# Attention output with V stationary and row sums apart, and the other arm of the final branch laid out next

## The chip, the cores and the metric

The kernel runs on one core of one Trainium2 chip. The metric is device time in microseconds (us) of one execution. A core has TensorE (PE, matmuls into PSUM), VectorE (DVE), ScalarE (ACT), GpSimd (POOL) and SyncE (SP, which issues most DMAs). Each runs its own instruction stream in order, and semaphores tie them together.

## The reference

One transformer block on 2048 tokens of width 1024, in bf16, with adaptive layer norm. Six vectors of 1024 come from `silu(c) @ w_mod`. There are 32 query heads and 4 key/value heads of 128; keys and values are the last W = 512 positions of a cache.

```python
h = _layernorm(x) * (1 + ca) + sa
q = (h @ wq), in 32 heads of 128
scores = einsum('bhqd,bhkd->bhqk', q, k) * 128 ** -0.5     # k: 512 positions, each kv head serves 8 heads
p = softmax(scores)
o = einsum('bhqk,bhkd->bhqd', p, v)
x = x + ga * (o, heads side by side) @ wo
h = _layernorm(x) * (1 + cb) + sb
x = x + gb * ((silu(h @ w_gate) * (h @ w_up)) @ w_down)     # inner width 3584
```

## The kernel before

There are two programs in one. `fast_path` computes everything with a softmax that subtracts no maximum, and beside it a bound on the scores; where the bound is too large a flag is set, and `general_path` computes the output again. The flag is read by every engine at the end (lines 1241 to 1243) and the usual value, 0, skips `general_path`.

`fast_path` cuts the 2048 tokens into four chunks of 512 columns. The attention stage is one loop (line 1203) over k = 0 to 128, where unit g is head g % 32 of chunk g // 32. In step k the program issues the scores of unit k (`emit_s`, line 1025), the query projection of unit k + 3 (`emit_q`, line 1015), whatever tasks a table holds for step k (`at`, line 806; filled in lines 1114 to 1147), and last the attention output of unit k - 1 (`emit_o`, line 1054). The tasks are layer norms, modulation rows, loads, the bound, and the output projection `emit_wo` (line 1090), one 128x512 result a step, from 13 steps after the first head of its group of eight on. The instruction order on each engine follows from this; a scheduler may move instructions that are not pinned.

Matmuls: `emit_q` 8 with 512 moving columns; `emit_s` 4, each 128 positions against 512 tokens, in two PSUM tiles of two banks, with one exponential on ACT for each into `pT` (512 positions by 512 tokens, positions on partitions); `emit_wo` 8.

`emit_o` takes each 128x128 block of `pT` as the stationary operand and lets V move: 128 columns of V and one column of ones (`v_sb` is loaded with room for it, lines 705 to 709). So 16 matmuls of 129 columns a head leave tokens on partitions, and column 128 holds the sum of the probabilities. Three results of 129 share a PSUM bank (`SLOTS`); `close_bank` (line 1042) takes the reciprocals of the sums and writes the scaled output as bf16 into `oq`. `xpose_o` (line 1077) turns `oq` by four DMA transposes a group of four heads, issued by SP, into `oT`, with the head's 128 values on partitions, which `emit_wo` uses as stationary operand.

Tiles of 512 columns in PSUM come from one ring of four banks (`mm`, line 649). In SBUF, pool `blkC` (line 634, 13 tiles) holds `oq`, `oT`, the `wo` tiles, and later the `wd` tiles of the down projection; `blkB` (7) holds `wq`, kT, `v_sb`, and later `wg` and `wu`; all weights are loaded by SP in program order (`load`, line 666).

After the attention stage come, for each chunk, 28 steps of gate and up (`emit_gu`, line 1161) and 8 of down (`emit_down`, line 1181). Line 779 is a form that matters below: the modulation rows as matmuls with 32 stationary columns, four of them to the four quarters of a bank's partitions.

Of the kernel before, what the change touches and what calls it, by code (L numbers as in the profile page):

```python
# [8 lines left out]
ACT = mybir.ActivationFunctionType  # L9
ALU = mybir.AluOpType  # L10
AX = mybir.AxisListType
BF16 = mybir.dt.bfloat16
FP32 = mybir.dt.float32
# [575 lines left out]
def fast_path(ctx, tc, flag, A_x, A_k_cache, A_v_cache, A_wq, A_wo, B_x, B_w_gate, B_w_up,  # L589
# [3 lines left out]
    nc = tc.nc  # L593
    P = 128
    _, S, D = A_x.shape
    _, Hkv, Sk, Dh = A_k_cache.shape
    HD = A_wq.shape[1]
    H = HD // Dh
# [4 lines left out]
    TCW = 512  # L603
    NTC = S // TCW
    QT = TCW // P
    DT = D // P
    FT = F // P
    WT = W // P
    DH = D // 512
    HQ = 8  # L610
    NQ = H // HQ
    NFG = FT // 4
    scale = float(Dh) ** -0.5
# [13 lines left out]
    v_v = A_v_cache[0][:, k0:k0 + W, :].rearrange("kv (j p) d -> p kv j d", p=P)  # L627
# [3 lines left out]
    hpool = ctx.enter_context(tc.tile_pool(name="hT", bufs=4))  # L631
    pa_ = ctx.enter_context(tc.tile_pool(name="blkA", bufs=8))
    pb_ = ctx.enter_context(tc.tile_pool(name="blkB", bufs=7))
    pc_ = ctx.enter_context(tc.tile_pool(name="blkC", bufs=13))
    wk = ctx.enter_context(tc.tile_pool(name="work", bufs=2))
    sm = ctx.enter_context(tc.tile_pool(name="small", bufs=4))
    psp = ctx.enter_context(tc.tile_pool(name="psum", bufs=4, space=bass.MemoryType.PSUM))
    dp = ctx.enter_context(tc.tile_pool(name="dram", bufs=4, space=bass.MemoryType.DRAM))

    def blkA(name, shape, dt=BF16):  # L640
        return pa_.tile(shape, dt, name=name, tag="A")

    def blkB(name, shape, dt=BF16):
        return pb_.tile(shape, dt, name=name, tag="B")

    def blkC(name, shape, dt=BF16):
        return pc_.tile(shape, dt, name=name, tag="C")

    def mm(name, shape=(P, 512), dt=FP32):
        return psp.tile(list(shape), dt, name=name, tag="mm", bufs=4)  # L650

    def big(name, shape=(P, 2, 512), dt=FP32):
        return psp.tile(list(shape), dt, name=name, tag="s", bufs=2)
# [6 lines left out]
    def pin(ins, what="steps"):  # L660
        return tc.keep_in_program_order(ins) if stage[what] else ins

    def fetch(out, in_):
        pin(nc.sync.dma_start(out=out, in_=in_), "dma")  # L664

    def load(out, in_):
        with nc.allow_non_contiguous_dma(reason="weight slice"):
            fetch(out=out, in_=in_)
# [20 lines left out]
    def load_wq(cc, hg, parts=(0, 1)):  # L689
        for i in parts:  # L690
            t = blkB("wq", [P, 4, 512])
            load(t, wq_v[:, 4 * i:4 * i + 4, hg * 512:(hg + 1) * 512])
            wq_tiles[(cc, hg, i)] = t
# [8 lines left out]
    for kv in range(Hkv):  # L702
        pin(nc.sync.dma_start_transpose(
            out=kT[:, kv, :], in_=A_k_cache[0, kv, k0:k0 + W, :]), "dma")
    VW = Dh + 4
    v_sb = blkB("v_sb", [P, Hkv, WT, VW])
    for kv in range(Hkv):
        load(v_sb[:, kv, :, 0:Dh], v_v[:, kv])
    nc.gpsimd.memset(v_sb[:, :, :, Dh:VW], 1.0)
    load_wq(0, 1)  # L710


# [2 lines left out]
    ones_bf = const.tile([P, P], BF16, name="ones_bf")  # L715
# [90 lines left out]
    def at(k, f, *a):  # L806
        tasks.setdefault(k, []).append((f, a))
# [115 lines left out]
    for t in range(QT):  # L923
        ln_stats(t)
        n = ln_norm(t, t % 2 == 0)
# [5 lines left out]
    for half in range(DH):  # L931
# [6 lines left out]
        for n in range(4 * LEAD):  # L938
            dt, g = (4 * half + n // LEAD, n % LEAD) if half == 0 else (4 + n % 4, n // 4)
            nc.tensor.matmul(q0_ps[g],  # L940
                             lhsT=wq_tiles[(0, 0, dt // 4)][:, dt % 4, g * P:(g + 1) * P],
                             rhs=hT[("h1", 0)][:, dt, :], start=(dt == 0), stop=(dt == DT - 1))
# [7 lines left out]

    def bound_wq(hg, i, j):
        w = wq_tiles[(1 + hg % (NTC - 1), hg, i)][:, 2 * j:2 * j + 2, :]
        junk = wk.tile([P, 2, 512], BF16, name="junk", tag="junk", bufs=1)
        col = (hg * 2 + i) * 2 + j
        pin(nc.vector.scalar_tensor_tensor(out=junk, in0=w, scalar=1.0, in1=w, op0=ALU.mult,
                                           op1=ALU.mult, accum_out=sq[:, col:col + 1]))
# [8 lines left out]
    def bound_k(kv):  # L965
        for j in range(WT):
            i = kv * WT + j
            junk = wk.tile([P, Dh], BF16, name="junk", tag="junk", bufs=1)
            src = k_ld[0][:, kv, j, :]
            pin(nc.vector.scalar_tensor_tensor(out=junk, in0=src, scalar=1.0, in1=src,  # L970
                                               op0=ALU.mult, op1=ALU.mult,
                                               accum_out=kk[:, i:i + 1]))
# [35 lines left out]
    NU = NTC * H  # L1008
    pT = {}
    oT = {}  # L1010
    oq = {}
    acc = {}
    wo_tiles = {}

# [10 lines left out]
    def emit_s(g):  # L1025
        kv = (g % H) // rep
        p = blkA("pT", [P, WT, TCW])
        for jj in range(WT // 2):
            s_ps = big("s_ps")
            for i in range(2):  # L1030
                j = 2 * jj + i
                nc.tensor.matmul(s_ps[:, i, :], lhsT=kT[:, kv, j * P:(j + 1) * P], rhs=qT[g],  # L1032
                                 start=True, stop=True)
            nc.scalar.activation(out=p[:, 2 * jj:2 * jj + 2, :], in_=s_ps, func=ACT.Exp,  # L1034
                                 scale=scale)
        del qT[g]
        pT[g] = p

    SLOTS = 3
    o_slot = {"n": 0, "runs": []}  # L1040

    def close_bank():
        ps, runs = o_slot["ps"], o_slot["runs"]
        n = o_slot["n"]
        rl = sm.tile([P, SLOTS], FP32, name="rl", tag="rl", bufs=4)
        nc.vector.reciprocal(out=rl[:, 0:n], in_=ps[:, 0:n, Dh])
        for g, t0, t1, s0 in runs:
            cnt = t1 - t0
            dst = oq[(g // H, (g % H) // 4)][:, t0:t1, g % 4, :]
            sc = rl[:, s0:s0 + cnt].unsqueeze(2).to_broadcast([P, cnt, Dh])  # L1050
            nc.vector.tensor_tensor(out=dst, in0=ps[:, s0:s0 + cnt, 0:Dh], in1=sc, op=ALU.mult)  # L1051
        o_slot.update(n=0, runs=[])

    def emit_o(g):
        cc, h = divmod(g, H)
        kv = h // rep
        if h % 4 == 0:
            oq[(cc, h // 4)] = blkC("oq", [P, QT, 4, Dh])
        for t in range(QT):
            if o_slot["n"] == 0:  # L1060
                o_slot["ps"] = mm("o_ps", (P, SLOTS, Dh + 1))
            s_ = o_slot["n"]
            for j in range(WT):
                nc.tensor.matmul(o_slot["ps"][:, s_, :], lhsT=pT[g][:, j, t * P:(t + 1) * P],  # L1064
                                 rhs=v_sb[:, kv, j, 0:Dh + 1], start=(j == 0),
                                 stop=(j == WT - 1))
            runs = o_slot["runs"]
            if runs and runs[-1][0] == g:
                runs[-1][2] = t + 1
            else:  # L1070
                runs.append([g, t, t + 1, s_])
            o_slot["n"] = s_ + 1
            if o_slot["n"] == SLOTS or (t == QT - 1 and h % HQ == HQ - 1):
                close_bank()
        del pT[g]

    def xpose_o(cc, hg):
        src = oq.pop((cc, hg))
        dst = oT[(cc, hg)] = blkC("oT", [P, 4, TCW])
        for t in range(QT):  # L1080
            pin(nc.sync.dma_start_transpose(
                out=dst[:, :, t * P:(t + 1) * P],
                in_=src[:, t, :, :].rearrange("p h d -> p (h d)")), "dma")

    def load_wo(cc, q, dh, i):
        t = blkC("wo", [P, 4, 512])
# [27 lines left out]
    for n, vecs in enumerate(((2, 4), (5, 3))):  # L1114
        for part in range(2):
            k = 16 * n + 8 * part
# [5 lines left out]
    for tt in range(QT, S // P):  # L1122
        cc, t = divmod(tt, QT)
# [8 lines left out]
    at(NU - H + 29, bound_mod)  # L1132
    at(NU + 3, bound_final)
    for g in range(3, NU, 4):
        at(g + 3, xpose_o, g // H, (g % H) // 4)
    for cc in range(1, NTC):
        plan_ln((cc - 1) * H + (10 if cc == 1 else 2), ("h1", cc), ca1, sa)
    for cc in range(NTC):
        for q in range(NQ):
            s0 = cc * H + q * HQ + HQ + 5  # L1140
# [13 lines left out]
    def load_gu(cc, fg):  # L1154
        for nm, v in (("wg", wg_v), ("wu", wu_v)):
            for i in range(2):
                t = blkB(nm, [P, 4, 512])
                load(t, v[:, 4 * i:4 * i + 4, fg * 512:(fg + 1) * 512])
                gu_w[(cc, fg, nm, i)] = t
# [38 lines left out]
    def run_tasks(k):  # L1198
        for f, a in tasks.pop(k, ()):
            f(*a)  # L1200

    stage["steps"] = True
    for k in range(NU + 1):
        if k % 4 >= 2 and 4 * (k // 4) + 8 < NU:
            g = 4 * (k // 4) + 8
            load_wq(g // H, (g % H) // 4, (k % 4 - 2,))
        if k < NU:
            emit_s(k)
        if k + LEAD < NU:
            emit_q(k + LEAD)  # L1210
        if k == NU - 4:
            load_gu(0, 0)
        run_tasks(k)
        if k >= 1:
            emit_o(k - 1)
    stage.update(dma=False, steps=False)
    for cc in range(NTC):
# [18 lines left out]
def kernel(tc, *args):  # L1236
    nc = tc.nc
    with tc.tile_pool(name="guard", bufs=1) as gp:
        flag = gp.tile([1, 1], I32, name="flag")
        fast_path(tc, flag, *args)  # L1240
        over = nc.values_load(flag[0:1, 0:1], min_val=0, max_val=1)
        with tc.If(over > 0):
            general_path(tc, *args)


# [28 lines left out]
```

## Time and profile before

| what | value |
|---|---|
| time, median of 3 runs | 1288.97 us (1285.7 to 1289.6) |
| the profiled execution | 1289.6 us, span 1287.8 us, mean TensorE clock 0.996 |
| PE waits, all kinds | 9.7 us |
| attention stage | about 30 to 677 us |
| gate, up and down of the four chunks | about 677 to 1283 us |
| costliest PE groups (starts to starts, share of the chain that ended last) | gu_ps 29%, a_ps 17%, q_ps 17%, d_ps 15%, o_ps 9%, s_ps 8% |
| last matmul, last DVE operation, end | 1282.6, 1283.2, 1287.8 us |

The span is from the first instruction to the last, and the time of the execution is a little longer. A group line gives line, engine, operation, `out<-in`, shapes and count, then busy time and the mean of one in ns, then the idle time ahead of it. Matmuls are pipelined: the mean of one (379 ns for 512 columns) is longer than the step from one start to the next, so costs are read from starts. A line of the waits names the waiting engine and line, the releaser, and the total in us, the count and the longest. PEq, ACTq and so on are the sequencers of the engines, which run branches and semaphores.

### The profile page before, as it was taken

The numbers are of one execution on the slowest core, as the hardware profiler recorded it, in microseconds if no ns is written. First come the engines' busy times: TensorE is split into PE (matmuls) and PEld (weight loads), VectorE is DVE, ScalarE is ACT, GpSimd is POOL, SyncE is SP. The second block draws the span as 40 slices with busy tenths as digits, with TensorE's granted clock in tenths as the row PEclk, the third lists the DMA queues.
The fourth block names the chain that finished last, engine by engine and source line by source line (L and its number), as shares of the span: only waits on it lengthen the run. The fifth ranks groups of instructions, "written<-read, shape, count | busy, mean of one in ns | idle before, by whom it ended". The sixth has DMA issues, their size and how long they took to land.

```text
span 1287.8 us, 18140 instructions
## 1 busy us (share of the span) xinstructions
PE 1272.8 (99%) x7601; PEld 644.0 (50%) x7601; DVE 577.8 (45%) x1271; ACT 334.0 (26%) x433; POOL 1.3 (0%) x8
## 2 busy tenths in 40 slices
PE   7999999999999999999999999999999999999998
PEld 4555555555555555555554444444444444444444
DVE  4464557866577755576663641221122121222122
ACT  3543334343333433333341111011100111011100
POOL 0000000000000000000000000000000000000000
PEclk9999999999999999999999999999999999999999
DMA  9878465456345654445578475453536445354401
GB/s 295 264 196 221 169 148 171 133 144 203 96 123 156 148 140 147 116 147 131 132 186 257 134 218 171 135 192 132 179 103 219 152 152 175 135 192 132 147 18 34
DMA packets 280107, 204.20 MB, mean 159 GB/s; under 512 B 113865, under 2 KB 273609, under 8 KB 280018
## 3 DMA queue, kind: packets, MB, share of 16 engines
q1 hardware_dynamic: 275106, 198.78, 52.2%
q10 hardware_dynamic: 4912, 4.20, 1.0%
q8 instruction: 61, 1.00, 0.3%
q14 instruction: 28, 0.23, 0.1%
HBM read 174.08 MB, written 4.21 MB: 138 GB/s over the span
## 4 chain that ended last, share of the span: by engine, by line
PE 95%; DMA 2%; DVE 1%; SPq 1%; ACT 0%; issue 0%; DVEq 0%
PE gu_ps L1168 29%; PE a_ps L1096 17%; PE q_ps L1019 17%; PE d_ps L1188 15%; PE o_ps L1064 9%; PE s_ps L1032 8%; DMA wm<-in_w_mod_dram 1%; SPq L664 1%; DMA modT<-row_d 0%; DMA hT<-xn 0%; DMA wu<-in_B_w_up_dram 0%; PE row_ps L779 0%; PE q_ps L940 0%; DVE st L816 0%; SPq L848 0%; ACT pT L1034 0%
## 5 line engine op out<-in xcount | busy, mean ns | idle before, releaser
L1034 ACT ACTIVATE pT<-s_ps 128x1024 bf16<-128x1024 f32 x256 | 248.6, 1020 | 345.4 <-PE s_ps L1032 345.4
L1096 PE MATMUL a_ps<-wo,oT 128*128 128x512 bf16 x1024 | 241.9, 379 | 1.0 <-DVE acc L1102 1.0
L1019 PE MATMUL q_ps<-hT,wq 128*128 128x512 bf16 x1000 | 237.3, 380 | 0.3 <-DVE modT L755 0.3
L1168 PE MATMUL gu_ps<-hT,wu 128*128 128x512 bf16 x896 | 212.3, 380 | 2.1 <-DMA wu<-in_B_w_up_dram 2.1
L1168 PE MATMUL gu_ps<-hT,wg 128*128 128x512 bf16 x896 | 212.9, 381 | 0.0
L1174 DVE TENSOR_TENSOR guT<-gu_ps,sg 128x512 bf16<-128x512 f32 x112 | 77.4, 691 | 285.5 <-ACT sg L1173 285.5
L1173 ACT ACTIVATE sg<-gu_ps 128x512 bf16<-128x512 f32 x112 | 66.9, 597 | 492.6 <-PE gu_ps L1168 492.6
L1188 PE MATMUL d_ps<-wd,guT 128*128 128x512 bf16 (+2 forms) x952 | 194.2, 366 | 0.0
L916 DVE CAST qT<-q_ps 128x512 bf16<-128x512 f32 x128 | 88.2, 690 | 179.0 <-PE q_ps L1019 176.8
L1096 PEld LDWEIGHTS <-oT 128*128 128x128 bf16 x1024 | 99.9, 98 | 122.3 <-issue 2.1
L1019 PEld LDWEIGHTS <-wq 128*128 128x128 bf16 x1000 | 97.9, 98 | 117.9 <-issue 0.5
L1064 PEld LDWEIGHTS <-pT 128*128 128x128 bf16 x2048 | 128.4, 97 | 30.6 <-issue 0.4
L1188 PEld LDWEIGHTS <-guT 128*128 128x128 bf16 x952 | 90.9, 98 | 103.0
L1168 PEld LDWEIGHTS <-wu 128*128 128x128 bf16 x896 | 87.8, 98 | 108.7 <-DMA wu<-in_B_w_up_dram 2.6
L1168 PEld LDWEIGHTS <-wg 128*128 128x128 bf16 x896 | 87.9, 98 | 106.1 <-issue 1.1
L1064 PE MATMUL o_ps<-v_sb,pT 128*128 128x129 bf16 x2048 | 139.2, 219 | 0.0
L1032 PE MATMUL s_ps<-qT,kT 128*128 128x512 bf16 x512 | 131.3, 378 | 0.6 <-ACT pT L1034 0.6
L1051 DVE TENSOR_TENSOR oq<-o_ps,rl 128x256 bf16<-128x256 f32 (+2 forms) x256 | 101.3, 420 | 4.3
L1192 DVE TENSOR_TENSOR f<-d_ps,gb_bc 128x512 f32<-128x512 f32 (+2 forms) x34 | 22.4, 660 | 147.1 <-PE d_ps L1188 147.1
L1104 DVE TENSOR_TENSOR acc<-a_ps,acc 128x512 f32<-128x512 f32 x64 | 44.1, 688 | 40.8 <-PE a_ps L1096 40.8
L1032 PEld LDWEIGHTS <-kT 128*128 128x128 bf16 x512 | 44.7, 97 | 31.9 <-issue 1.3
L816 DVE BATCH_NORM_STATS2 st<-x 128x6 f32<-128x512 bf16 x64 | 41.3, 680 | 2.7 <-DMA x<-in_A_x_dram 2.5
(75 smaller groups left out, 306.7 us busy)
## 6 DMA issues: line engine op xcount, KB each, us to landing
wq<-in_A_wq_dram SPq DMA_DIRECT2D x64, 512.0 KB, 4.8
wo<-in_A_wo_dram SPq DMA_DIRECT2D x64, 512.0 KB, 5.5
wg<-in_B_w_gate_dram SPq DMA_DIRECT2D x56, 512.0 KB, 5.0
wu<-in_B_w_up_dram SPq DMA_DIRECT2D x56, 512.0 KB, 5.6
wd<-in_B_w_down_dram SPq DMA_DIRECT2D x56, 512.0 KB, 7.2
wmr<-in_w_mod_dram SPq DMA_DIRECT2D x8, 1024.0 KB, 8.6
x<-in_A_x_dram SPq DMA_DIRECT2D x16, 256.0 KB, 5.1
wm<-in_w_mod_dram SPq DMA_DIRECT2D x4, 1024.0 KB, 10.7
```

The lines of the kernel that those rows point to most:

```text
L916: nc.vector.tensor_copy(out=t, in_=q_ps)
L1019: nc.tensor.matmul(q_ps, lhsT=wq_tiles[(cc, h // 4, dt // 4)][:, dt % 4, (h % 4) * P:(h % 4 + 1) * P], rhs=hT[("h1", cc)][:, dt, :], start ...
L1032: nc.tensor.matmul(s_ps[:, i, :], lhsT=kT[:, kv, j * P:(j + 1) * P], rhs=qT[g], start=True, stop=True)
L1034: nc.scalar.activation(out=p[:, 2 * jj:2 * jj + 2, :], in_=s_ps, func=ACT.Exp, scale=scale)
L1051: nc.vector.tensor_tensor(out=dst, in0=ps[:, s0:s0 + cnt, 0:Dh], in1=sc, op=ALU.mult)
L1064: nc.tensor.matmul(o_slot["ps"][:, s_, :], lhsT=pT[g][:, j, t * P:(t + 1) * P], rhs=v_sb[:, kv, j, 0:Dh + 1], start=(j == 0), stop=(j == W ...
L1096: nc.tensor.matmul(a_ps, lhsT=oT[(cc, 2 * q + i)][:, hh % 4, t * P:(t + 1) * P], rhs=wo_tiles[(cc, q, dh, i)][:, hh % 4, :], start=(hh == ...
L1104: nc.vector.tensor_tensor(out=acc[(cc, t)][:, dsl], in0=a_ps, in1=acc[(cc, t)][:, dsl], op=ALU.add)
L1168: nc.tensor.matmul(ps[:, n, :], lhsT=gu_w[(cc, fg, nm, dt // 4)][:, dt % 4, fi * P:(fi + 1) * P], rhs=hT[("h2", cc)][:, dt, :], start=(dt ...
L1173: nc.scalar.activation(out=g, in_=ps[:, 0, :], func=ACT.Silu)
L1174: nc.vector.tensor_tensor(out=guT[(cc, fg)][:, fi, :], in0=ps[:, 1, :], in1=g, op=ALU.mult)
L1188: nc.tensor.matmul(d_ps, lhsT=guT[(cc, f // 4)][:, f % 4, t * P:(t + 1) * P], rhs=wd_tiles[(cc, dh, f // 4)][:, f % 4, c0:c0 + w], start=( ...
```

## The change

Four things change in `fast_path`, and one in the function that calls both programs.

- `emit_o` takes V (128 positions by 128 values) as stationary operand and `pT` as the moving one: 4 matmuls of 512 columns a head. The result has the head's values on partitions, as `oT` needs it; ACT copies it there without scaling. `oq`, `close_bank`, `xpose_o` and the ones column go.
- The sums: in `emit_s`, DVE adds the four blocks of `pT` to one (`psA`, then `psB`). `emit_l`, every fourth step ahead of `emit_o`, sums over partitions with four matmuls of 32 ones columns each into the quarters of a bank; ACT makes the reciprocal by a logarithm and an exponential, and the four rows go to DRAM.
- `load_rb` (a task one step later) reads them back to all partitions as two fp32 tiles, and `emit_norm` (two more steps later) multiplies `oT` by them in place, on DVE.
- `blkC` has 10 tiles in place of 13, and the scratch tiles of the bound share the buffers of `psA`.
- The branch asks for the arm that is not taken into `general_path` as the next block. In the built program this arm (waits and additions on semaphores, 2 to 9 instructions an engine) then follows the compare, and ends with a jump to the program's end; `general_path` lies between. Before, `general_path` followed the compare, and the arm lay behind it, next to the end.

```diff
-    pc_ = ctx.enter_context(tc.tile_pool(name="blkC", bufs=13))
+    pc_ = ctx.enter_context(tc.tile_pool(name="blkC", bufs=10))
...
-    VW = Dh + 4
-    v_sb = blkB("v_sb", [P, Hkv, WT, VW])
+    v_sb = blkB("v_sb", [P, Hkv, WT, Dh])
...
+        a = wk.tile([P, 2, TCW], BF16, name="psA", tag="psA", bufs=2)
+        nc.vector.tensor_tensor(out=a, in0=p[:, 0:2, :], in1=p[:, 2:4, :], op=ALU.add)
+        b = wk.tile([P, TCW], BF16, name="psB", tag="psB", bufs=5)
+        nc.vector.tensor_tensor(out=b, in0=a[:, 0, :], in1=a[:, 1, :], op=ALU.add)
+        rec[g] = b
+
+    def emit_l(g):
+        l_ps = mm("l_ps")
+        for i in range(4):
+            nc.tensor.matmul(l_ps[32 * i:32 * i + 32, :], lhsT=ones_bf[:, 0:32],
+                             rhs=rec.pop(g - 3 + i), start=True, stop=True)
+        r = wk.tile([P, TCW], FP32, name="rinv", tag="f32", bufs=2)
+        nc.scalar.activation(out=r, in_=l_ps, func=ACT.Ln)
+        nc.scalar.activation(out=r, in_=r, func=ACT.Exp, scale=-1.0)
+        d = dp.tile([4, TCW], FP32, name="r_d", tag="r_d", bufs=4)
+        nc.scalar.dma_start(out=d, in_=r[0:P:32, :])
+        rinv[g // 4] = d
+
+    def load_rb(g):
+        d = rinv[g // 4]
+        rinv[g // 4] = []
+        for i in range(2):
+            rb = wk.tile([P, 2, TCW], FP32, name="rb", tag="rb", bufs=2)
+            fetch(out=rb, in_=d[2 * i:2 * i + 2, :].partition_broadcast(P))
+            rinv[g // 4].append(rb)
+
+    def emit_norm(g):
+        o = oT[(g // H, (g % H) // 4)]
+        for i, rb in enumerate(rinv.pop(g // 4)):
+            oo = o[:, 2 * i:2 * i + 2, :]
+            pin(nc.vector.tensor_tensor(out=oo, in0=oo, in1=rb, op=ALU.mult))
 
     def emit_o(g):
...
+        o_ps = mm("o_ps")
+        for j in range(WT):
+            nc.tensor.matmul(o_ps, lhsT=v_sb[:, kv, j, :], rhs=pT[g][:, j, :],
+                             start=(j == 0), stop=(j == WT - 1))
+        nc.scalar.copy(out=oT[(cc, hg)][:, hi, :], in_=o_ps)
...
     for g in range(3, NU, 4):
-        at(g + 3, xpose_o, g // H, (g % H) // 4)
+        at(g + 2, load_rb, g)
+        at(g + 4, emit_norm, g)
...
         if k >= 1:
+            if k % 4 == 0:
+                emit_l(k - 1)
             emit_o(k - 1)
...
-        with tc.If(over > 0):
+        with tc.If(over > 0, preferred_fallthrough_block=False):
             general_path(tc, *args)
```

More of the change, by code (lines that the diff above doesn't have):

```diff
@@ L704, in fast_path @@
             out=kT[:, kv, :], in_=A_k_cache[0, kv, k0:k0 + W, :]), "dma")
-    VW = Dh + 4
-    v_sb = blkB("v_sb", [P, Hkv, WT, VW])
+    v_sb = blkB("v_sb", [P, Hkv, WT, Dh])
     for kv in range(Hkv):
-        load(v_sb[:, kv, :, 0:Dh], v_v[:, kv])
-    nc.gpsimd.memset(v_sb[:, :, :, Dh:VW], 1.0)
+        load(v_sb[:, kv], v_v[:, kv])
     load_wq(0, 1)
@@ L952, in bound_wq @@
         w = wq_tiles[(1 + hg % (NTC - 1), hg, i)][:, 2 * j:2 * j + 2, :]
-        junk = wk.tile([P, 2, 512], BF16, name="junk", tag="junk", bufs=1)
+        junk = wk.tile([P, 2, 512], BF16, name="junk", tag="psA", bufs=2)
         col = (hg * 2 + i) * 2 + j
@@ L967, in bound_k @@
             i = kv * WT + j
-            junk = wk.tile([P, Dh], BF16, name="junk", tag="junk", bufs=1)
+            junk = wk.tile([P, Dh], BF16, name="junk", tag="psA", bufs=2)
             src = k_ld[0][:, kv, j, :]
@@ L1010, in fast_path @@
     oT = {}
-    oq = {}
+    rec = {}
+    rinv = {}
     acc = {}
@@ L1037, in emit_s @@
         pT[g] = p
[L1039 to L1052, printed above, removed]
+        a = wk.tile([P, 2, TCW], BF16, name="psA", tag="psA", bufs=2)
[26 more added lines that the diff above has]
+            pin(nc.vector.tensor_tensor(out=oo, in0=oo, in1=rb, op=ALU.mult))
     def emit_o(g):
@@ L1056, in emit_o @@
         kv = h // rep
[L1057 to L1074, printed above, removed]
-        del pT[g]
[L1077 to L1083, printed above, removed]
+        hg, hi = h // 4, h % 4
+        if hi == 0:
+            oT[(cc, hg)] = blkC("oT", [P, 4, TCW])
+        o_ps = mm("o_ps")
[3 more added lines that the diff above has]
+        nc.scalar.copy(out=oT[(cc, hg)][:, hi, :], in_=o_ps)
+        del pT[g]
     def load_wo(cc, q, dh, i):
```

## The prediction

> **What bounds the kernel now.** I read the waits of the matmul engine first, then its timeline in one head of the attention stage, the vector engine's groups, and last the branch at the end of the program.
>
> The page and PE's waits:
>
> ```profile
> PE 1272.8 (99%) x7601; PEld 644.0 (50%) x7601; DVE 577.8 (45%) x1271; ACT 334.0 (26%) x433; POOL 1.3 (0%) x8
> ```
>
> ```profile
> PE mod_ps L753 <- DMA wm<-in_w_mod_dram: 2.5, 2, 1.4
> PE gu_ps L1168 <- DMA wu<-in_B_w_up_dram: 2.1, 1, 2.1
> ```
>
> These are its two largest waits; all ten kinds together make 9.7 us of 1287.8. So the time is the sum of what PE issues, and an edit counts by what it adds to or takes from that stream, or by a new wait in it. The timeline of PE in one steady head:
>
> ```profile
> 308.00 1.02 PE L1032 MATMUL s_ps<-qT,kT 128*128 128x512 bf16 x4
> 308.87 1.89 PE L1019 MATMUL q_ps<-hT,wq 128*128 128x512 bf16 x8
> 310.59 1.89 PE L1096 MATMUL a_ps<-wo,oT 128*128 128x512 bf16 x8
> 312.32 1.09 PE L1064 MATMUL o_ps<-v_sb,pT 128*128 128x129 bf16 x16
> 313.24 0.59 PE L1032 MATMUL s_ps<-qT,kT 128*128 128x512 bf16 x2
> ```
>
> The first column is the start; difference of starts is what a group costs. Eight matmuls with 512 columns take 1.73 us, 0.216 each; sixteen with 129 columns 0.92, 0.058 each. A head takes 5.24 us, with no gap.
>
> **The output matmuls.** Removed: 16 matmuls of 129 columns a head, 0.92 us. Added: 4 of 512 columns, 4 x 0.216 = 0.86. Gain 0.06 a head, 128 heads: **-7.5 us**. (16 x 129 = 2064 columns against 2048; the rest of the gain is the fixed part of twelve matmuls.) Weight loads fall from 2048 to 512; they lie under matmuls now and then.
>
> **The row sums.** The ones column gave the denominators with the output. Now each four heads issue four matmuls with 32 stationary columns, one to each quarter of the partitions, moving 512. The trace has this form in the modulation rows, sixteen at a time:
>
> ```profile
> 161.74 1.24 PE L1019 MATMUL q_ps<-hT,wq 128*128 128x512 bf16 x5
> 162.91 1.05 PE L779 MATMUL row_ps<-wmr,sil 128*32 128x512 bf16 x16
> 163.89 1.90 PE L1096 MATMUL a_ps<-wo,oT 128*128 128x512 bf16 x8
> 165.63 1.08 PE L1064 MATMUL o_ps<-v_sb,pT 128*128 128x129 bf16 x16
> ```
>
> The five q matmuls from 161.74 would end their turn at 161.74 + 5 x 0.216 = 162.82; the next stream starts at 163.89 and its eight take 1.74 instead of 1.73. So sixteen cost 1.08 us, four rounds of four side by side. Three rounds at 0.216 leave 1.08 - 0.65 = 0.43 us for a round that comes alone: 0.22 of work and about 0.2 for going from 128x128 to 128x32 and back. 32 groups x 0.43 = **+13.6 us**; bounds 32 x 0.22 = 7 (the change of shape free) and 32 x 0.86 = 28 (the four one after another, against which the row speaks). Net of PE's stream: +6.1, between -0.5 and +20.
>
> **The vector engine.** Its groups:
>
> ```profile
> L1051 DVE TENSOR_TENSOR oq<-o_ps,rl 128x384 bf16<-128x384 f32 x80 | 44.4, 555 | 2.1
> L1051 DVE TENSOR_TENSOR oq<-o_ps,rl 128x256 bf16<-128x256 f32 x96 | 40.0, 419 | 1.1
> L1046 DVE RECIPROCAL rl<-o_ps 128x3 f32<-128x3 f32 x160 | 25.8, 165 | 0.0
> L955 DVE SCALAR_TENSOR_TENSOR junk<-wq 128x1024 bf16<-128x1024 bf16 x32 | 38.9, 1215 | 0.0
> L835 DVE TENSOR_SCALAR xn<-x,mv 128x1024 bf16<-128x1024 bf16 x26 | 14.0, 540 | 0.0
> ```
>
> ```profile
> 205.00:250.00 45.00, 45.00 (x311) 24.70 (x310) 37.56 (x80) 17.14 (x21) 0.00 (x0) 1.00 0.50 140
> ```
>
> (the window's columns: length, busy of PE, weight loads, DVE, ACT, POOL, then clock, DMA share, GB/s.) Removed with the 128-wide pieces and reciprocals: 101.3 + 28.3 us, 1.01 a head. Added a head: an add of 128x1024 bf16, one of 128x512, and half a multiply of 128x1024 by fp32 factors. No row is an add of two bf16 tiles in SBUF. The nearest are L835 (one tile, 0.54) and L955 (two tiles, with an accumulated sum, 1.22); for 512 wide 0.41 (L856) and 0.69 (L1194, fp32). The multiply, with fp32, goes by L955: 1.22, 0.61 a head. Together 1.56 to 2.52 a head; I take the middle of each pair, 0.88 + 0.55 + 0.61 = 2.04, since the add has two tiles but no accumulated sum: +1.03 a head.
>
> Most heads have room: 62% busy over the 660 us of attention. The hot stretch above, 37.56 of 45 us or 4.37 a head, goes to 4.9 to 5.9, against a head of 5.24 - 0.06 + 0.11 = 5.29. At the upper end DVE falls behind by 0.6 a head over 8.6 heads, 5 us; the like stretches 390 to 435 (35.86 busy) and 540 to 585 (33.77) give 3.4 and 1.3, so 0 to 10 us in all; with the middle values the first lacks 1 us and the others nothing, and a pair of multiplies (2.4 us) beside a sum of squares (1.2) comes in bursts. What covers it: q is made three heads ahead, and PE's four 512-wide banks pass to the next user after about a head. What is late next is a bank that waits for its copy by DVE. I take **+2 us**.
>
> [...]
>
> **Hidden parts.** Copying the output from PSUM moves to ACT: 0.6 a head by L1173 (128x512, 597 ns), and a logarithm and an exponential of that width per four heads, 0.3 a head; ACT, 38% busy in the hot stretch and 51% in the first chunk (31.65 of 62 us), stays under 90% in that chunk's 3.5 us heads. The factors then go out to DRAM and come back as two 512 KB broadcasts. From rows: 0.4 + 1.2, a small DRAM write 3.9 (gd_d), a broadcast 5.2 (ga_bc) and about 2 for the second: 12.7 us from the row sums to the multiply, which is due three heads later, 15.8 us, or 10.5 in the first thirteen heads. There DVE may sit 2 us in front of the multiply, with qT copies queued behind it; three heads of lead cover that. If the cover is gone, PE waits that 2 us, three times. SP loses 128 transposes (1.26 us of its queue each) and gains 64 broadcasts that hold wq and wo behind them for at most a head; wo is loaded five heads ahead. blkC with 10 tiles in place of 13 holds 5 oT and 5 wo at its fullest. In the down stage four wd loads instead of one wait for the pass before: issued 0.86 apart, each due 6.04 + 1.73 = 7.77 us after it; loads so spaced landed in 3.9, 5.6, 6.1 and under 7.1 us. Zero, with 0.7 us to spare.
>
> **The end.** The branch:
>
> ```profile
> L1242 SPq EVENT_SEMAPHORE  x8: 17/17/17, 1261.5 to 1285.4; - x8
> L1242 SPq COMPARE_BRANCH  x1: 53/53/53, 1253.5 to 1253.5; - x1
> L1242 DVEq COMPARE_BRANCH  x1: 76/76/76, 1283.6 to 1283.6; - x1
> L1242 ACTq COMPARE_BRANCH  x1: 54/54/54, 1284.2 to 1284.2; - x1
> L1242 DVEq EVENT_SEMAPHORE  x1: 21/21/21, 1286.5 to 1286.5; - x1
> L1242 ACTq EVENT_SEMAPHORE  x1: 17/17/17, 1286.9 to 1286.9; - x1
> ```
>
> ACT jumps over the general path at 1284.2 and runs its next instruction at 1286.9: 2.7 us; DVE 2.9. SP jumped at 1253.5, unseen, and then waited for the last output to land, 1285.4. After the change the usual block comes first, but in the built program its own last instruction is a jump to the program's end, which still lies behind the general path. So ACT and DVE jump as far as before, and SP jumps after that landing: 1285.4 + 2.8 + 0.7 (its final waits, 1285.4 to 1287.0 less the 0.9 it waited for DVE and ACT) + 0.8 (to 1287.8) = 1289.7: **+2.0 us**. Bounds: -0.9 if a jump without condition costs nothing on any engine, +2.7 with PE's 3.6 us jump.
>
> [...]
>
> **Sum.** The profiled execution took 1289.6 (span 1287.8, 1.8 around it), 0.6 above the median 1288.97. 1289.6 - 7.5 + 13.6 + 2 + 2.0 = 1299.7; less 0.6: **1299**.
>
> **Rivals.**
> - *DVE becomes the bound*: adds at 1.22 and 0.69. +6.1 + 2.0 + 10 = 1307. For it: 83% busy now in the hot stretch; against it, the packed rows L835. Chance 0.2.
> - *Late factors*: with the trip out and back at 20 us, not 12.7, DVE sits 4 us before each multiply and PE waits about 0.5 in each of 32 groups: +16, 1315. For it, 0.7 DMA share in the first chunk; against, 0.5 later. 0.07.
> - *Not slower*: the change of shape is free, since the four matmuls share one set of ones, so a group costs 0.22; PE then nets -0.5 and the end stays within 0 to 2: 1288 to 1291. It decides from a group under 0.28 us with DVE keeping up. Against it, L779 pays at both its ends. 0.11.
> - *The branch does what it says* and jumps vanish on all engines: 2.9 less than forecast, 1296, which lies inside the forecast's own range.
> - *Faster*: both of the last two at once, and the transposes that SP loses end PE's stall on wu near 755 (2.1 us and the slow matmuls behind it): 1284. 0.04.
>
> Forecast 1295 to 1303: 0.58. Faster by over 0.3% (3.9 us, what a measurement here can tell from no change) 0.04, within it 0.11, slower 0.85. Range 1291 to 1311: it leaves out half of the not slower case, the faster one and most of the late one, 0.16.
>
> **What would show it.** Row-sum groups that delay the next stream by 0.43; o_ps at 0.86 a head; SP resuming 2.7 us or more after the last landing. Wrong if PE has waits for DVE of over 10 us, or if a group costs 0.22.

## The result and the profile after

| | before | after |
|---|---|---|
| time, median of 4 runs | 1287.34 us (1285.61 to 1289.6) | 1296.47 us (1294.76 to 1297.0) |
| profiled execution | 1289.6, span 1287.8 | 1296.92, span 1295.1 |
| start of the first gate matmul (end of attention) | 677.46 | 682.64 |
| end of the last matmul | 1282.58 | 1287.69 |
| from there to the end of the span | 5.24 | 7.44 |

After over before is 1.0068, with an interval of 1.0045 to 1.009: slower. Two stretches of the span grew: attention by 5.2 us, and what lies behind the last matmul by 2.2 us. The feed-forward part between them took as long as before (gate and up matmuls 390.7 and 390.6 us by their starts, down matmuls 193.5 in both).

First the page of the changed kernel and the complete list of what PE waited for (engine and line <- what released it: us in all, times, longest):

```profile
PE 1280.3 (99%) x6193; PEld 577.9 (45%) x6193; DVE 653.1 (50%) x1159; ACT 433.7 (33%) x625; POOL 1.2 (0%) x7
```

```profile
PE gu_ps L1168 <- DMA wu<-in_B_w_up_dram: 2.0, 1, 2.0
PE mod_ps L751 <- DMA wm<-in_w_mod_dram: 2.0, 2, 1.2
PE warm_ps L725 <- POOL warm_w L719: 1.5, 1, 1.5
PE h_ps L925 <- ACT xn L830: 0.8, 1, 0.8
PE s_ps L1031 <- ACT pT L1033: 0.6, 2, 0.3
PE q_ps L1018 <- DVE modT L753: 0.3, 1, 0.3
PE mod_ps L751 <- DVE modT L753: 0.3, 1, 0.3
```

PE still is 99% busy and waits 7.5 us in all, less than before. No wait is for a sum, a factor or a multiply; the only DVE tile in the list, modT, belongs to the modulation. DVE has 75 us more to do and ACT 100 us more, and PE notices neither. A wait that the list of before had, 1.0 us of a_ps for DVE's acc near 92 us, is gone.

The timeline of PE in the changed kernel, around one group of row sums (start, length, operation):

```profile
306.47 1.89 PE L1095 MATMUL a_ps<-wo,oT 128*128 128x512 bf16 x8
308.29 0.40 PE L1048 MATMUL l_ps<-psB,ones_bf 128*32 128x512 bf16 x4
308.62 1.04 PE L1079 MATMUL o_ps<-pT,v_sb 128*128 128x512 bf16 x4
309.49 1.03 PE L1031 MATMUL s_ps<-qT,kT 128*128 128x512 bf16 x4
```

Eight a matmuls take 1.73, so their turn ends at 308.20; o starts at 308.62. The four row sums with both changes of shape cost 0.42. The o matmuls after them take 0.87 by starts, 0.86 in heads without sums.

DVE's new groups (busy us, mean ns of one | idle before them), and its hottest stretch (length, busy us of PE, weight loads, DVE, ACT, POOL):

```profile
L1038 DVE TENSOR_TENSOR psA<-pT 128x1024 bf16<-128x1024 bf16 x128 | 87.8, 686 | 89.0 <-ACT pT L1033 88.9
L1069 DVE TENSOR_TENSOR oT<-oT,rb 128x1024 bf16<-128x1024 bf16 x64 | 75.4, 1218 | 1.8 <-DMA rb<-r_d 1.8
L1040 DVE TENSOR_TENSOR psB<-psA 128x512 bf16<-128x512 bf16 x128 | 53.3, 417 | 0.6
```

```profile
208.00:253.00 45.00, 45.00 (x214) 20.02 (x213) 43.30 (x74) 23.10 (x33) 0.00 (x0) 1.00 0.62 156
```

A head costs DVE 0.686 + 0.417 + 1.218/2 = 1.71 us. In the hot stretch it is busy 43.30 of 45 us where it was 37.56, and PE still has no gap. The factors were late twice, by 1.8 us together.

The branch in the changed kernel (ns min/median/max, first and last start in us), and below it the first lines behind its target:

```profile
L1244 SPq EVENT_SEMAPHORE  x8: 17/17/17, 1267.9 to 1290.9; - x8
L1244 SPq COMPARE_BRANCH  x2: 38/48/57, 1261.2 to 1291.0; - x2
L1244 ACTq COMPARE_BRANCH  x2: 38/44/51, 1289.3 to 1289.5; - x2
```

```profile
L1271 SPq EVENT_SEMAPHORE  x14: 17/28/28, 1293.5 to 1295.1; - x14
...
L1271 ACTq DRAIN  x2: 8/44/80, 1292.1 to 1294.6; - x2
```

Each engine now has two entries: the compare, which falls through, and the jump that closes the usual block. ACT jumps at 1289.5 and runs its next instruction at 1292.1, as far as before. SP, which used to jump 32 us earlier, now waits for the last output to land (1290.9), jumps at 1290.99 and goes on at 1293.50: 2.51 us, in which SP runs nothing. What moves in that time is told by the list of DMA queues for 1291 to 1293.5 us (packets, MB, share of the 16 engines), which has these four packets of instructions and no others:

```profile
q14 instruction: 3, 0.02, 3.7%
q8 instruction: 1, 0.02, 2.4%
```

The last output also lands later. SP's last wait starts 2.8 us behind the last matmul before (1285.4 and 1282.58) and 3.2 after (1290.92 and 1287.69), so 0.4 of the 2.2 us stands ahead of SP's jump.

### The profile page after: what moved, and what is told of

The parts are those of the page before. It is cut to its first block, busy times and chain, and to the rows that moved or that the text cites. A ratio compares the mean times of both kernels' runs of the same rounds, so it can differ in the third digit from the quotient of the medians.

```text
span 1295.1 us, 15444 instructions
## 1 busy us (share of the span) xinstructions
PE 1280.3 (99%) x6193; PEld 577.9 (45%) x6193; DVE 653.1 (50%) x1159; ACT 433.7 (33%) x625; POOL 1.2 (0%) x7
## 4 chain that ended last, share of the span: by engine, by line
PE 97%; DMA 1%; DVE 1%; SPq 0%; ACT 0%; issue 0%; DVEq 0%
PE gu_ps L1168 29%; PE a_ps L1095 17%; PE q_ps L1018 17%; PE d_ps L1188 15%; PE o_ps L1079 9%; PE s_ps L1031 8%; PE l_ps L1048 1%; DMA wm<-in_w_mod_dram 1%; PE q_ps L938 0%; DMA hT<-xn 0%; DMA wu<-in_B_w_up_dram 0%; PE row_ps L777 0%; PE mod_ps L751 0%; SPq L664 0%; ACT pT L1033 0%; PE h_ps L925 0%
## 5 line engine op out<-in xcount | busy, mean ns | idle before, releaser
L1033 ACT ACTIVATE pT<-s_ps 128x1024 bf16<-128x1024 f32 x256 | 252.0, 1026 | 72.8 <-PE s_ps L1031 70.1
L1018 PEld LDWEIGHTS <-wq 128*128 128x128 bf16 x1000 | 97.6, 98 | 118.4 <-DMA wq<-in_A_wq_dram 0.7
L1038 DVE TENSOR_TENSOR psA<-pT 128x1024 bf16<-128x1024 bf16 x128 | 87.8, 686 | 89.0 <-ACT pT L1033 88.9
L1079 PE MATMUL o_ps<-pT,v_sb 128*128 128x512 bf16 x512 | 131.7, 380 | 0.0
L1081 ACT CAST oT<-o_ps 128x512 bf16<-128x512 f32 x128 | 74.5, 582 | 166.1 <-PE o_ps L1079 166.1
L1031 PEld LDWEIGHTS <-kT 128*128 128x128 bf16 x512 | 50.1, 98 | 61.5 <-issue 1.5
L1069 DVE TENSOR_TENSOR oT<-oT,rb 128x1024 bf16<-128x1024 bf16 x64 | 75.4, 1218 | 1.8 <-DMA rb<-r_d 1.8
L1079 PEld LDWEIGHTS <-v_sb 128*128 128x128 bf16 x512 | 47.4, 98 | 60.4 <-issue 7.7
```

Source lines behind the costliest of these rows:

```text
L1018: nc.tensor.matmul(q_ps, lhsT=wq_tiles[(cc, h // 4, dt // 4)][:, dt % 4, (h % 4) * P:(h % 4 + 1) * P], rhs=hT[("h1", cc)][:, dt, :], start ...
L1038: nc.vector.tensor_tensor(out=a, in0=p[:, 0:2, :], in1=p[:, 2:4, :], op=ALU.add)
L1069: pin(nc.vector.tensor_tensor(out=oo, in0=oo, in1=rb, op=ALU.mult))
L1079: nc.tensor.matmul(o_ps, lhsT=v_sb[:, kv, j, :], rhs=pT[g][:, j, :], start=(j == 0), stop=(j == WT - 1))
L1081: nc.scalar.copy(out=oT[(cc, hg)][:, hi, :], in_=o_ps)
```

## The experiments

The theory after the result: the row sums' 0.43 a group, less 0.06 a head, make the attention slower; SP's jump at the end adds the rest; DVE's added work is covered. The rivals: DVE holds PE up; or the end is slower because of something other than the layout of the branch. Each ratio is over the kernel before, on the same chip, with its 95% interval.

**after_old_branch**: the changed attention with the old layout of the branch (5 rounds).

```
-        with tc.If(over > 0, preferred_fallthrough_block=False):
+        with tc.If(over > 0):
```

> The changed kernel with the branch as it was, so that the general path follows the compare again. Exit theory (SP's jump over the general path, exposed behind the last landing, is what the new layout adds): the time from the last matmul to the end goes from 7.4 back to 5.2 us and the PE stream stays, so a span of 1292.9, 2.2 below the changed kernel, ratio to before 1.004. Rival (the longer tail comes with the new attention code, not with the layout): the tail stays at 7.4, span 1295.1, ratio 1.006.

Measured: 1293.36 us, 1.0054 [1.004, 1.0068]. From the last matmul to the end 5.18 us (7.44 with the new layout); SP's final waits run from 1289.24, at once on the landing, since its jump lies at 1259.9. The attention change alone costs 6.9 us [5.1, 8.7].

**before_new_branch**: the attention of before, with only the branch laid out anew (5 rounds).

```
-        with tc.If(over > 0):
+        with tc.If(over > 0, preferred_fallthrough_block=False):
```

> The kernel before with only the branch changed. Exit theory: tail 7.4 in place of 5.2, span 1290.0, ratio 1.0017. Rival (the layout does what it says and the usual case no longer jumps): the jumps of ACT and DVE go, the tail falls to 4.3, span 1286.9, ratio 0.9993. Rival (layout does nothing): 1.000.

Measured: 1289.25 us, 1.0022 [1.0013, 1.0031], that is 2.8 us; from the last matmul to the end 7.80 us (5.24 before). SP's branches and the first lines behind its target, in this kernel:

```profile
L1242 SPq COMPARE_BRANCH  x2: 43/48/53, 1251.7 to 1284.4; - x2
```

```profile
L1269 SPq EVENT_SEMAPHORE  x14: 17/28/28, 1286.9 to 1288.5; - x14
```

The same 2.5 us behind the last landing (1284.38 to 1286.91), with none of the attention changed. Laying the branch out anew makes the kernel slower by itself. That settles the second rival. The jump is not all of it: SP's last wait starts 3.6 us behind the last matmul here, where it starts 2.8 behind it in the kernel before and in after_old_branch. The runs show that this comes with the layout, but not why.

**no_sums**: leaves out the row sums (both adds, the ones matmuls, the factors and the multiply), so its output is not normalised (3 rounds).

```
-        a = wk.tile([P, 2, TCW], BF16, name="psA", tag="psA", bufs=2)
-        nc.vector.tensor_tensor(out=a, in0=p[:, 0:2, :], in1=p[:, 2:4, :], op=ALU.add)
-        b = wk.tile([P, TCW], BF16, name="psB", tag="psB", bufs=5)
-        nc.vector.tensor_tensor(out=b, in0=a[:, 0, :], in1=a[:, 1, :], op=ALU.add)
-        rec[g] = b
...
-        at(g + 2, load_rb, g)
-        at(g + 4, emit_norm, g)
+        pass
...
-            if k % 4 == 0:
-                emit_l(k - 1)
```

> The changed kernel without the row sums: no adds, no sum matmuls, no reciprocals, no trip through DRAM, no multiply, so its output is not normalised. PE stream theory (a group of four sum matmuls costs 0.43 us of PE, and all the rest of the row sums is hidden): 32 x 0.43 = 13.7 less, span 1281.4, ratio 0.995. Rival (the change of shape is free, a group costs 0.22): 7 less, span 1288. Rival (the adds, the copies on ACT or the DMAs slow PE as well): clearly more than 13.7 less.

Measured: 1282.33 us, 0.9964 [0.995, 0.9977], span 1281.3. The first gate matmul starts at 668.69, against 682.64: the sums cost 13.9 us, 0.43 for each of 32 groups. By starts, 10.7 of it stands with l_ps, 2.7 with the a matmuls ahead of it (the stream that the change of shape ends) and 0.4 with the o matmuls behind. If DVE's adds or the multiply held PE up, this difference would be above 32 x 0.43 (the price by the timeline above, and by l_apart below), and it isn't.

**add_twice**: the 128x1024 add is made twice, 0.69 us more for DVE in every head, 88 in all (3 rounds).

```
-        nc.vector.tensor_tensor(out=a, in0=p[:, 0:2, :], in1=p[:, 2:4, :], op=ALU.add)
+        for _ in range(2):
+            nc.vector.tensor_tensor(out=a, in0=p[:, 0:2, :], in1=p[:, 2:4, :], op=ALU.add)
```

> [...] Theory of the prediction (DVE has room on average, and in the hot stretches lead and banks cover what it lacks): by the sum of rows the stretches lack 4, 2.5 and 0 us, of which the cover takes most: 0 to 3 us more, with PE waits that name DVE only there. Rival (DVE is the bound as soon as it is loaded this much): 7 us or more. Rival (DVE never matters): 0.

Measured: 1298.07 us, 1.0091 [1.0076, 1.0107], span 1296.0 against 1295.1. New in the list of PE's waits:

```profile
PE o_ps L1080 <- ACT rinv L1052: 0.7, 1, 0.7
PE o_ps L1080 <- DVE f L1108: 0.7, 1, 0.7
...
PE o_ps L1080 <- DVE acc L1102: 0.2, 1, 0.2
```

and the hot stretch of this kernel:

```profile
208.00:253.00 45.00, 44.09 (x207) 19.73 (x209) 44.48 (x77) 22.38 (x33) 0.00 (x0) 1.00 0.63 156
```

The three waits stand in the o matmuls right behind a group of row sums, at 246, 437 and 628 us: the two of 0.7 us in the first two hot stretches, the one of 0.2 behind the third. Only two of them, 0.9 us, are DVE's. The other names ACT's logarithm, and rightly: in the built program this one o_ps, of the 32 behind a group, lies in the bank of the l_ps just ahead of it, and it starts as the logarithm has read that (437.94 and 437.89). In the first stretch DVE is busy 44.48 of 45 us, all that there is, and PE loses 1.6 us in 660 by all three waits. The first gate matmul is 2.5 us later than in the changed kernel; 0.7 of that was there at the first s matmul, ahead of attention, where PE waited longer for wm (3.3 against 2.0 us). The span grew by less, 0.9 us: the changed kernel's profiled execution has 3.4 us at a granted clock of 0.5 behind its wait for wu near 763 us, and add_twice's has none there (gate and up matmuls 388.8 us by starts instead of 390.6). So the DVE work that the change adds is short of the point where it bounds, and even past it the loss is small. That settles the first rival.

**l_together and l_apart**: what makes a group cost 0.43? Both add a second group of four matmuls of the same form on a constant tile, whose result is not used; l_together puts it right behind each group, l_apart two heads later (3 rounds each).

```
+    def dup_l():
+        l2 = mm("l2_ps")
+        for i in range(4):
+            tc.keep_in_program_order(
+                nc.tensor.matmul(l2[32 * i:32 * i + 32, :], lhsT=ones_bf[:, 0:32], rhs=warm_w,
+                                 start=True, stop=True))
...
                 emit_l(k - 1)
+                dup_l()          # l_together
+            if k % 4 == 2:
+                dup_l()          # l_apart
```

> The changed kernel with a second group of four sum matmuls (on a constant tile, into a bank that nobody reads) straight behind each sum group. Shape theory (0.22 of the 0.43 us of a group is work, the rest is paid for going to the 32 column form and back): the second group pays only its work, 32 x 0.216 = 6.9 more, span 1302.0. Rival (0.43 is what a group costs wherever it stands): 13.8 more, span 1308.9.

> The same extra groups, but two steps after the sum group, between 512 wide matmuls of the usual form. Shape theory: each pays the change of form too, 32 x 0.43 = 13.8 more, span 1308.9. Rival (a group costs its work, 0.22, and the changed kernel's 0.43 came from waiting for DVE's adds): 6.9 more, span 1302.0.

Measured: l_together 1302.72 us, 1.0126 [1.0109, 1.0142], first gate matmul 6.76 us later than in the changed kernel, 0.21 a group. l_apart 1310.65 us, 1.0175 [1.0158, 1.0192], 13.87 us later, 0.43 a group. The timelines, l_together first:

```profile
309.05 1.89 PE L1102 MATMUL a_ps<-wo,oT 128*128 128x512 bf16 x8
310.87 0.40 PE L1048 MATMUL l_ps<-psB,ones_bf 128*32 128x512 bf16 x4
311.09 0.39 PE L1061 MATMUL l_ps<-warm_w,ones_bf 128*32 128x512 bf16 x4
311.42 1.04 PE L1086 MATMUL o_ps<-pT,v_sb 128*128 128x512 bf16 x4
```

```profile
301.81 1.89 PE L1102 MATMUL a_ps<-wo,oT 128*128 128x512 bf16 x8
303.63 0.40 PE L1061 MATMUL l_ps<-warm_w,ones_bf 128*32 128x512 bf16 x4
303.96 1.04 PE L1086 MATMUL o_ps<-pT,v_sb 128*128 128x512 bf16 x4
```

The second group of l_together starts 0.22 after the first: its four matmuls run side by side, in the time of one. In l_apart the lone group costs what a group of row sums costs, with nothing to wait for (its operand is constant). The same four matmuls cost 0.21 without the change of shape and 0.43 with it, so the change to 32 columns and back costs 0.22 us a time. It has two ends: after the a matmuls the next stream starts 0.09 late, and after the group the o matmuls start 0.33 behind its start, where its work takes 0.21 to 0.22.

**after_tiny and before_tiny**: does SP's late jump cost anything when its target is near? In place of the general path, which the usual case doesn't run, the untaken arm holds a copy of one row (3 rounds each; after_tiny has the new layout, before_tiny the old).

```
-            general_path(tc, *args)
+            nc.sync.dma_start(out=args[-1].flatten_outer_dims()[0:1, :],
+                              in_=args[0].flatten_outer_dims()[0:1, :])
```

> The changed kernel with a one row copy in place of the general path, so that the jump to the end is short; with the flag set the output would be wrong, with the usual flag nothing is left out. Distance theory (the jumps cost because their target lies 30 KB and more away): SP's jump behind the last landing takes 0.1 to 0.5 in place of 2.5 us, tail 5.0 to 5.4, span 1292.7 to 1293.1. Rival (a jump costs the same however far, or the layout costs through its extra instructions): tail stays 7.4, span 1295.1.

> The kernel before with the same one row copy in place of the general path. Distance theory: ACT and DVE no longer resume 2.7 and 2.9 us after their branches, and the end is set by the last landing: tail 4.5 in place of 5.2, span 1287.1. Rival (distance does not matter): tail 5.2, span 1287.8.

Measured: after_tiny 1291.19 us, 1.0033 [1.0023, 1.0043], from the last matmul to the end 3.02 us; before_tiny 1285.09, 0.9989 [0.9979, 0.9998], 3.37 us. Both fell below what was expected (5.0 to 5.4, and 4.5). The reason: the one-row copy touches little, so the branch came ahead of the last pieces of the output in every queue, and the end of this kernel is no longer the end of the other with a shorter jump. For ACT in after_tiny, for instance:

```profile
L1244 ACTq COMPARE_BRANCH  x2: 38/43/48, 1285.7 to 1285.8; - x2
```

and its next instruction, one of an output piece, starts at 1285.98, 0.17 us after the jump at 1285.81. So the totals say only that the order of the arms no longer matters there (3.0 and 3.4 us); the price of distance is read from the single jump, 0.17 us near and 2.6 far on the same engine. Whether a late near jump of SP would cost nothing was not shown: here it wasn't late. Two more readings bear on distance. From its last matmul to its end after_tiny has no packet on the instruction queues and before_tiny one; the changed kernel has eight there, the kernel before six. And POOL, which jumps over the general path too, goes on 0.45 us after its jump in the changed kernel and 0.15 after it in after_tiny; in the built program its part of that path is about 60 instructions, SP's 493 and ACT's 1988. So it is the far targets that cost here, 2.5 to 3.3 us in the changed kernel; what such a jump waits for was not shown, and how the price grows with distance, or from what distance on, no run took.

Between the two tiny kernels lie about 6.1 us (their intervals leave nearly 2 either way), what the changed attention costs when both ends are nearly alike. That this meets the prediction's net for PE, +6.1, to the digit is chance: before_tiny holds a wait of 2.3 us for acc that the sum did not have.

## Why the prediction was right, and where it was off

The direction, the mechanism and the two large terms held; the time came 2.5 us under the forecast. Of these, 1.6 are the base, which no term could know: the forecast started from a median of 1288.97 for the kernel before, and with the fourth run that median is 1287.34. The rest is in the terms: in the profiled executions the change cost 7.3 us where the sum said 10.1.

- **Output matmuls, -7.5.** By starts o_ps takes 110.9 us where it took 118.4: -7.5.
- **Row sums, +13.6.** 13.9 by leaving them out. The reading of one row of sixteen (1.08 us less three rounds) gave 0.43 a group, split as 0.22 of work and about 0.2 for the shape; l_together and l_apart measured 0.21 and 0.22. The "not slower" rival needed a group under 0.28, with the four sharing the array for nothing; they do run side by side, but the change of shape is paid.
- **DVE's stall, +2: the mis-sized term; measured 0.** Two things were too dear. The adds were taken in the middle between L835 and L955, at 0.88 and 0.55; they took 0.686 and 0.417. The multiply with fp32 factors takes 1.218, near the 1.22 taken from L955. And the step from a DVE that falls behind to a PE that waits was too direct: by the prediction's own arithmetic (busy time of a head over 5.29, times 8.6 heads, in the three hot stretches) add_twice, with 2.40 us a head, should have cost 4.0 + 2.3 + 0.2 = 6.5 us; PE's new waits came to 1.6, of them 0.9 for DVE. That the lead of three heads pays for the delay, so that DVE catches up behind the stretch, fits this but no run took it alone.
- **A wait of before that went, -1.1; not in the sum.** PE's wait for acc near 92 us (a gap of 1.37 us in the starts, where 0.22 is usual) is missing after. DVE shows why. In the kernel before, the copy to acc stands behind modT, in front of which DVE sits 3.63 us until a DMA lands:

```profile
92.22 0.17 DVE L802 TENSOR_SCALAR modT<-modT 128x8 f32<-128x8 f32 x1 [3.63 <-DMA modT<-row_d]
92.90 0.67 DVE L1102 COPY acc<-a_ps 128x512 f32<-128x512 f32 x1
```

After the change the copy comes first:

```profile
92.08 0.68 DVE L1101 COPY acc<-a_ps 128x512 f32<-128x512 f32 x1
93.14 0.17 DVE L800 TENSOR_SCALAR modT<-modT 128x8 f32<-128x8 f32 x1 [0.38 <-DMA modT<-row_d]
```

The three kernels with the attention of before have both waits (DVE's 3.6, 3.9 and 5.0 us, PE's 1.0, 1.2 and 2.3), and no kernel with the new output matmuls has that wait of PE, no_sums included. The gain is a side effect of the new order of work, and the forecast had no part in it.

- **Hidden parts, 0.** ACT's copies, logarithms and exponentials caused no wait of PE; the factors made DVE wait 1.8 us in all, where 2 us a time were allowed in the first chunk; wd made no wait of PE in the changed kernel (0.9 us, once, in l_apart), and the wait for wu stayed (2.1 and 2.0).
- **The end, +2.0.** 2.2 by the profile, and 2.8 [1.7, 4.0] by the time of before_new_branch. (The terms of this step as printed end at 1289.7, 1.9 above 1287.8.) The step said that SP would now jump behind the last landing and pay a far jump: 2.51 us where 2.8 was taken, then 0.76 (0.7 taken) and 0.87 (0.8). These alone are 1.8 more than before; the other 0.4 is the later landing, which the step put at nothing, so that its total fits a little better than its parts. The branch's own records are 38 to 57 ns on ACT and SP, but the next instruction comes 2.5 us (SP) to 3.3 us (PE) later in the changed kernel. So on ACT and SP the price stands behind the record and not in it. Four packets of instructions move in SP's 2.51 us, and ACT's near jump of 0.17 us in after_tiny goes without any; that an engine waits for such packets was not shown.

By the terms as measured: -7.5 + 13.9 - 1.1 + 2.2 = 7.5; the first s matmul came 0.2 us earlier, which leaves the 7.3 that the two profiled executions differ by. The repeated runs have 8.8 us for the whole change [5.8, 11.6] and 6.9 + 2.8 for its two parts, the same within their intervals.

No complete kernel of these beats the one before; no_sums and before_tiny, which do, leave work out. To gain, the sums would have to cost less than 7.5 us, 0.23 a group with the old layout of the branch (8.6 and 0.27 with the wait that went): the work alone is 0.21, so most of the change of shape would have to vanish. Sums for eight heads at once were not tried; by these numbers they would cost 16 x (0.22 + 2 x 0.21) = 10 us, still more than the output matmuls give.

## What to carry to other kernels

Where PE is 99% busy, count the changes of the array's shape as well as the columns: four matmuls that run side by side in the time of one (0.22 us, l_together) here cost that time twice when they came alone (0.43, l_apart). Of a branch at a program's end, ask on each engine which jump comes last and what it stands behind; the untaken compare saved nothing here, where the block that falls through must jump over the other arm after the last DMA has landed (2.51 us of SP in the changed kernel, 2.8 us of the time in before_new_branch). And whether an engine near its limit holds up another is tested cheaply by doubling one of its operations: what that costs says how much room was left (here 1.6 us of PE's waits, 0.9 of them for DVE, at 88 us more work of DVE).

## What the runs showed of the hardware

- Going from 128x128 matmuls to 32-column ones and back costs 0.22 us (0.43 a group in l_apart, 0.21 in l_together), 0.09 of it going in and the rest coming out; four 32-column matmuls on the four quarters take 0.21 to 0.22 us together (l_together), as one 128x128 matmul with 512 moving columns does (0.216).
- The same kind of jump costs ACT 0.17 us to a near target (after_tiny) and 2.6 to a far one (the changed kernel). To far targets SP takes 2.5, DVE 2.9 and PE 3.3 in the changed kernel; in before_new_branch DVE takes 3.75 and PE 3.7. During SP's 2.5 us four packets of instructions come in by DMA. POOL, with a short path to jump over, takes 0.45 in the changed kernel.
- The new layout of the branch also moved the landing of the last output, from 2.8 us behind the last matmul to 3.2 (the changed kernel) and 3.6 (before_new_branch); why is open.
- In add_twice DVE was filled to 44.48 of 45 us in one stretch, and PE, which is fed by it, waited 0.9 us for it in 660.
